# Forward steps taken in pairs, with finer fillers, and 16 small writes moved to another queue

## The chip, the cores and the metric

One core of a Trainium2 chip runs the whole program. The metric is the device time of one execution in microseconds (us); lower is better. The engines are PE (matrix products), DVE (VectorE), ACT (ScalarE, here mostly exponentials), POOL (GpSimd) and SP (SyncE, which here only issues DMAs). Each runs its own instructions in order, and they wait for each other through semaphores.

## What is computed

The reference runs a forward function of two halves and its gradients, in bfloat16, with 2048 positions, width 448 and 16 heads of 28.

```python
# A: linear attention
phi = lambda t: where(t > 0, t + 1, exp(t)) + 1e-6
kv = einsum("bhsd,bhse->bhde", phi(k), v);  z = sum over s of phi(k)
a  = (phi(q) @ kv / (phi(q) . z + 1e-6)) @ wo
# B: softmax attention, 16 query heads, one key and value head
p  = softmax(q @ k.T * 28 ** -0.5);  b = (p @ v) @ wo
out = concatenate([a, b]);  also the gradients of out with respect to all eight inputs, for grad_out
```

## The kernel before

**Forward of B.** The 2048 x 2048 scores of 16 heads are walked in 256 steps, one for each of 4 query blocks of 512, 4 groups of 4 heads, and 16 key tiles of 128 (`steps`, line 872). A step has these parts. `pe_s` (L876; its products are recorded at the helper's line, L105) makes half of a step's scores: two products of 32 rows each, on separate strips of the PE array, into one of two score buffers in PSUM. `act_e` (L888) is the exponential of one half, 128 x 1024, on ACT; a step has two. `pe_o` (L909; recorded at L108) adds the step's four products with the values into `oacc`, on separate column strips, and then issues, on SP's queue, the write of the step's exponentials `e` (512 KB) to DRAM, where the backward reads them again. `e` has five buffers. After every sixteenth step the sum is copied out, and `o_tail` turns it around and divides by the softmax's denominator; after every 64th, `queue_mid` (L930) adds the output product of that query block, the incoming gradient's product and its transposes.

**The order in a step** is written out by hand (L1103 on): both exponentials of step s, both halves of the scores of step s+1, the output products of step s-1, then `block`.

**Fillers.** The whole of the linear-attention half A is cut into pieces (`pieces_A`, L132), each a closure with a cost, close to its PE time in us. `block` (L1072) runs pieces from a list at the end of a step: it has a budget that grows by 1.15 a step up to 1.65, starts a piece while the budget is at least half its cost, and stops before a step's pieces go over the cap of 1.65. Pieces that come from B itself (`fillers`) go first, one a step. A's pieces run in this order: projections with their feature map, which adds exponentials on ACT (steps 17 to 51); the product of keys and input `G_part` (52 to 68); the third phase `p3_*`, output and inner gradients, with much DVE work (70 to 131), in it and behind it `gwo`, the gradient of A's output weight, summed over the four blocks; weight gradients `gw` of the queries (143 to 159); the fifth phase `p5_*`, the input's gradient (160 to 223); `gw` of the keys (224 to 240). Then the pools of A are released and the first tiles of the backward are loaded (`prefetch`).

**PSUM.** Two score buffers, one accumulator, three general buffers (`gen`) that all fillers share.

**DMA queues.** POOL and SP issue DMAs. In the last pass of `gwo` (L388 to 391), each of four groups is added up on DVE and written by four DMAs of 28 rows, 16 in all, on POOL's queue. On the same queue stand the output writes of B (`out_b_sb`, L961, two buffers), its saved output `onat_d` (L952) and A's writes. In the compiled program each DMA of a queue waits for a semaphore that it shares with the one issued eight before it on that queue.

**Backward of B.** 256 units with transposed reads of `e`; it follows the forward, and its code is not touched. A short part with B's weight gradients ends the program.

Of the kernel before, what the change touches and what calls it, by code (L numbers as in the profile page):

```python
# [16 lines left out]
DH = 28  # L17
D = 448
P = 128
# [5 lines left out]
def kernel(  # L25
# [21 lines left out]
    nc = tc.nc  # L47
# [36 lines left out]
    def mm(out_ap, lhsT, rhs, start=True, stop=True):  # L84
        nc.tensor.matmul(out_ap, lhsT=lhsT, rhs=rhs, start=start, stop=stop, tile_position=(0, 0))  # L85
# [46 lines left out]
    def pieces_A(gen, pl, post, flush, pre_tiles, pk_d, early):  # L132
        slabs, halves, w4, accp, chk, small, awk = pl
        out = []

        def piece(cost):
            def add(fn):
                out.append((cost, fn))
                return fn
            return add  # L140

# [234 lines left out]
        def gwo(qc, g):  # L376
            ps = gen([P, D], "gwo_ps")
            for b in range(4):
                mm(ps[:, :], V["onat"][:, qc * 4 + b, g * P:(g + 1) * P], V["ga", qc][:, b, 0:D], start=(b == 0),
                   stop=(b == 3))  # L380
            acc = V["gwo"][:, g, :]
            if qc == 0:
                nc.vector.tensor_copy(out=acc, in_=ps[:, :])
            elif qc < NQC - 1:
                nc.vector.tensor_tensor(out=acc, in0=ps[:, :], in1=acc, op=ALU.add)
            else:
                gsb = awk.tile([P, D], BF16, name="gwoA_sb", tag="osbA", bufs=4)
                nc.vector.tensor_tensor(out=gsb[:], in0=ps[:, :], in1=acc, op=ALU.add)  # L388
                for j in range(4):
                    h = 4 * g + j  # L390
                    nc.gpsimd.dma_start(out_3[h * DH:(h + 1) * DH, :], gsb[32 * j + 1:32 * j + 1 + DH, :])
            if g == 3 and qc < 2:
                ga_load(qc + 2)

# [14 lines left out]
        def part_pk2(k):  # L409
            nc.gpsimd.dma_start(V["onat"][:, 2 * k:2 * k + 2, :].rearrange("p t c -> p (t c)"),  # L410
                                pk_d[:, 1024 * k:1024 * k + 1024])
# [71 lines left out]
        def gw(src, c, q, bi):  # L483
            if q == 0:
                V["acc"] = gen([P, 512], "gw_acc")
            acc = V["acc"]
            for st in range(4 * q, 4 * q + 4):
                mm(acc[:, :], V["x"][:, st, c * P:(c + 1) * P], V[src][:, st, :], start=(st == 0), stop=(st == NS - 1))
            if q == 3:
                out_gw(acc, c, bi)  # L490

        def gw_all(c):
            for q in range(4):
                piece(0.86)(lambda c=c, q=q: gw("gq", c, q, 0))
                if c in (1, 2) and q % 2 == 1:
                    piece(0.0)(lambda k=2 + 2 * c + q // 2: part_pk2(k))

        for c in range(4):
            piece(0.25)(lambda c=c: gwv(c))
# [35 lines left out]
            piece(0.25)(lambda g=g: wT_tr("k", g))  # L535
        gw_all(3)

        def p5_dp(i):
            if i % 4 == 1 and i // 4 < 3:
                xT2(i // 4 + 1)  # L540
            ps = gen([P, 512], "ps_dpk")
            for c in range(4):
                mm(ps[:, :], V["xT", i // 4][:, i % 4, c, :], V["Wp"][:, c, :], start=(c == 0), stop=(c == 3))
            dph = awk.tile([P, 512], BF16, name="dph_A")
            nc.vector.tensor_scalar(out=dph[:], in0=V["pk"][:, i, :], scalar1=-1e-6, scalar2=1.0, op0=ALU.add,
                                    op1=ALU.min)
            gk = awk.tile([P, 512], BF16, name="gk_A", tag="gnd", bufs=4)
            nc.vector.tensor_tensor(out=gk[:], in0=ps[:, :], in1=dph[:], op=ALU.mult)
            V["gk", i] = gk

        def p5_tr(i):
            ps = gen([P, 1024], "qk_ps", BF16)
            tr4(ps, lambda g: V["gq"][:, i, g * P:(g + 1) * P])
            tr4(ps, lambda g: V["pk"][:, i, g * P:(g + 1) * P], 4)
            a = awk.tile([P, 1024], BF16, name="qkT_A", tag="t2k", bufs=4)
            nc.vector.tensor_copy(out=a[:], in_=ps[:, :])
            V["a", i] = a
# [10 lines left out]
        def p5_gx(i, k):  # L568
            a, b = V["a", i], V["b", i]
            if k == 0:  # L570
                V["gx"] = gen([P, D], "ps_gx")
            ps = V["gx"]
            lhs = (a[:, 0:512], b[:], a[:, 512:1024])[k]
            rhs = (V["wT", "q"], V["wT", "k"], V["Z"])[k]
            for g in range(4):
                mm(ps[:, :], lhs[:, g * P:(g + 1) * P], rhs[:, g, :], start=(k == 0 and g == 0),
                   stop=(k == 2 and g == 3))
            if k == 2:
                ot = awk.tile([P, D], BF16, name="gx_sb", tag="osbA", bufs=4)
                nc.vector.tensor_copy(out=ot[:], in_=ps[:, :])  # L580
                nc.gpsimd.dma_start(out1[i * P:(i + 1) * P, :], ot[:])
                del V["a", i], V["b", i]

        for i in range(NS + 2):
            if 0 <= i - 1 < NS:
                piece(0.45)(lambda i=i - 1: p5_tr(i))
            if i < NS:
                piece(0.86)(lambda i=i: p5_dp(i))
            if 0 <= i - 1 < NS:
                piece(0.25)(lambda i=i - 1: p5_tk(i))  # L590
            if 0 <= i - 2:
                for k in range(3):
                    piece(0.76)(lambda i=i - 2, k=k: p5_gx(i, k))
        for c in range(4):
            for q in range(4):
                if q % 2 == 0 and c < 4 and 2 * c + q // 2 in early:
                    piece(0.0)(early[2 * c + q // 2])
                piece(0.86)(lambda c=c, q=q: gw("pk", c, q, 1))
        return out

    ps = ExitStack()
# [267 lines left out]
    def e_rows(g, qc):  # L869
        return (g * NQC + qc) * S  # L870
# [17 lines left out]
    def act_e(h):  # L888
        s, hf = divmod(h, 2)
        if hf == 0:  # L890
# [2 lines left out]
                             in_=sps.pop(h)[:].rearrange("p j (a q) -> p j a q", a=4), func=ACT.Exp,  # L893
                             scale=scale)

    def o_tail(qc, g, osb):
        otp = gen([P, 4, P], "otp")
        for b in range(4):
            tpz(otp[:, b, :], osb[:, b * P:(b + 1) * P], identF)
        otv = otp[:].rearrange("p b (j c) -> p b j c", c=32)  # L900
        rl = rls[qc]
        nc.vector.reciprocal(out=rl[:, :, 4 * g:4 * g + 4], in_=otv[:, :, :, 0])
        for b in range(4):
            nc.vector.tensor_tensor(
                out=hv(onats[qc][:, b, g * P:(g + 1) * P]),
                in0=otv[:, b], in1=rl[:, b, 4 * g:4 * g + 4].unsqueeze(2).to_broadcast([P, 4, 32]),
                op=ALU.mult)

    def pe_o(s):  # L909
        qc, g, t = steps[s]  # L910
        if t == 0:
            oaccs[0] = psAcc.tile([P, 512], F32, name="oacc", tag="acc")
            if g == 0:
                onats[qc] = mid2.tile([P, 4, 512], BF16, name="onat_q")
                rls[qc] = mid2.tile([P, 4, H], F32, name="rl_q")
        oacc = oaccs[0]
        e = es.pop(s)
        for j in range(4):
            cmm(oacc[32 * j:32 * j + 32, :].rearrange("p (a q) -> p a q", a=4), vaug[:, t, :],
                e[:, :, j, :], j, t == 0, t == NS - 1)  # L920
        r0 = e_rows(g, qc) + t * P
        nc.sync.dma_start(edram[r0:r0 + P, :], e[:].rearrange("p a j q -> p (a j q)"))
        if t == NS - 1:
            osb = fwk.tile([P, 512], F32, name="osb")
            nc.vector.tensor_copy(out=osb[:], in_=oacc[:, :])  # L925
            posts.append(lambda: posts.append(lambda: fillers.insert(0, (1.0, lambda: o_tail(qc, g, osb)))))
            if g == 3:
                posts.append(lambda: posts.append(lambda: queue_mid(qc)))

# [142 lines left out]
    def block(rate, cap):  # L1072
        budget[0] = min(budget[0] + rate, cap)
        used = 0.0
        while True:
            q = peek()
            if q is None:
                return
            cost = q[0][0]
            if used > 0 and used + cost > cap or budget[0] < 0.5 * cost:  # L1080
                return
            if q is fillers:
                turn[0] += 1
            q.pop(0)[1]()
            budget[0] -= cost
            used += cost
# [16 lines left out]
    for s in range(NF):  # L1103
        turn[0] = 0
        act_e(2 * s)
        act_e(2 * s + 1)
        pend, posts[:] = posts[:], []
        for fn in pend:
            fn()
        pe_s(2 * s + 2)  # L1110
        pe_s(2 * s + 3)
        if s == NF - 1:
            pe_dp(0)
            pe_dp(1)
        if s > 0:
            pe_o(s - 1)
        block(1.15, 1.65)
        if apools.get("q") == []:
            prefetch(s)
    pe_o(NF - 1)  # L1120
    flush()
    flush()
# [229 lines left out]
```

## Time and profile before

| | |
|---|---|
| median of 3 runs | 1327.22 us (1321.48 to 1327.4) |
| the profiled execution | 1328.86 us, its span 1327.0 us |
| PE, ACT, DVE busy in the span | 1238.0, 1058.0, 938.4 us |
| forward, first to last exponential | 26.65 to 615.76 us, 256 steps |
| backward and end | from there to 1327.0 us |

The rows that carry the argument stand in the prediction. In a row of a group or a timeline the line (L105) is that of the program text, often of a helper; then come engine, operation, output<-inputs, count; in brackets or behind the bar stands the idle time of the engine just before, and what ended it. A row by stage gives each engine's busy time in that stretch with its count of instructions, then the granted PE clock (1.00 is full), the busy share of the DMA engines, and GB/s.

### The profile page before, as it was taken

The page shows a single profiled execution, that of the slowest core. Times are in us where ns is not written, and L with a number is a line of the kernel's source. Part 1 is how long each engine was busy: PE and PEld are TensorE (multiplying, and loading weights), DVE is VectorE, ACT ScalarE, POOL GpSimd, SP SyncE. Part 2 cuts the span into 40 slices and gives each one's busy share as a digit, 9 for nine tenths or more (in the row PEclk, how much of TensorE's full clock was granted, in tenths as well). Part 3 has the DMA queues.
Part 4 walks back from the last instruction along what each step waited for, and adds up shares of the span by engine and source line. Part 5 has one row for each costly group of instructions (what it writes and reads, how often), then busy time and mean ns, then how long its engine had stood idle before and what let it go on. Part 6 is the DMA issues. An engine that isn't in the chain of part 4 may idle for free.

```text
span 1327.0 us, 30124 instructions
## 1 busy us (share of the span) xinstructions
PE 1238.0 (93%) x12604; PEld 589.7 (44%) x12604; DVE 938.4 (71%) x1243; ACT 1058.0 (80%) x1174; POOL 213.9 (16%) x305
## 2 busy tenths in 40 slices
PE   6988998889789999998999999999999999999988
PEld 2322233444333343322555555554555555555544
DVE  6854338888553446212889999998999999999921
ACT  3899987888678888896888888887888888888830
POOL 6400301111411111100031111111111111111110
PEclk8999999999899999995999999998999999999989
DMA  6887798886877787799999999999999999999661
GB/s 171 313 269 280 273 300 302 296 294 264 281 274 293 268 280 296 285 325 309 205 221 206 218 232 222 220 217 224 221 218 220 221 223 217 220 223 218 130 210 46
DMA packets 626312, 322.00 MB, mean 243 GB/s; under 512 B 579120, under 2 KB 585008, under 8 KB 625920
## 3 DMA queue, kind: packets, MB, share of 16 engines
q1 hardware_dynamic: 615072, 291.30, 85.3%
q0 software_dynamic: 10080, 28.73, 6.7%
q8 instruction: 98, 1.61, 0.5%
q14 instruction: 38, 0.31, 0.1%
q10 hardware_dynamic: 1024, 0.05, 0.0%
HBM read 21.87 MB, written 153.45 MB: 132 GB/s over the span
## 4 chain that ended last, share of the span: by engine, by line
PE 66%; DVE 3%; DMA 3%; ACT 3%; issue 2%; POOL 0%; ACTq 0%; DVEq 0%; POOLq 0%
PE dsT_ps L89 19%; PE dp_ps L105 12%; PE akv L108 10%; PE s_ps L105 5%; PE dq_ps L108 4%; PE oacc L108 3%; PE ps_gx L85 3%; PE gw_acc L85 2%; ACT e L892 2%; PE ps_dpk L85 1%; PE gwq_acc L85 1%; ACT dsT L1167 1%; PE gwoB_ps L85 1%; PE ps_gxB L85 1%; DVE ds L1145 1%
## 5 line engine op out<-in xcount | busy, mean ns | idle before, releaser
L1167 ACT ACTIVATE dsT<-dsT_ps 128x1024 bf16<-128x1024 bf16 x512 | 497.5, 1028 | 101.5 <-PE dsT_ps L89 96.0
L892 ACT ACTIVATE e<-s_ps 128x1024 bf16<-128x1024 f32 x512 | 496.8, 1056 | 89.2 <-ACT e L892 50.2
L1145 DVE TENSOR_TENSOR ds<-dp_ps,eN 128x1024 bf16<-128x1024 f32 x336 | 393.1, 1217 | 32.6 <-PE dp_ps L105 24.7
L89 PE MATMUL dsT_ps<-identB,ds 128*128 128x128 bf16 x4096 | 282.5, 221 | 0.5 <-DVE ds L1145 0.2
L89 PEld LDWEIGHTS <-ds 128*128 128x128 bf16 x4096 | 234.5, 98 | 64.0 <-issue 59.9
L1145 DVE TENSOR_TENSOR ds<-dp_ps,eN_h 128x1024 bf16<-128x1024 f32 x176 | 207.0, 1216 | 13.5 <-PE dp_ps L105 7.9
L105 PE MATMUL s_ps<-qT_B,kT_rep 32*128 32x512 bf16 x1024 | 170.4, 398 | 38.6 <-ACT e L892 36.3
L105 PE MATMUL dp_ps<-vT_rep,doT_b 32*128 32x512 bf16 x768 | 151.3, 390 | 7.2 <-DVE ds L1145 6.5
L108 PE MATMUL akv<-ds,qn_b 128*32 128x512 bf16 x1024 | 157.2, 387 | 0.0
L1197 POOL TENSOR_TENSOR dkv<-dkv,asb 128x512 f32<-128x512 f32 x60 | 76.4, 1273 | 493.2 <-ACT asb L1196 493.2
L105 PEld LDWEIGHTS <-kT_rep 32*128 32x128 bf16 x1024 | 43.7, 91 | 166.2 <-issue 155.4
L108 PE MATMUL oacc<-e,vaug 128*32 128x512 bf16 x1024 | 106.3, 406 | 0.8 <-DVE osb L925 0.8
L105 PEld LDWEIGHTS <-doT_b 32*128 32x128 bf16 x768 | 37.1, 91 | 107.5 <-issue 84.3
L108 PE MATMUL akv<-eN,don_b 128*32 128x512 bf16 x512 | 78.4, 386 | 0.0
L108 PE MATMUL dq_ps<-dsT,kn 128*32 128x512 bf16 x1024 | 66.8, 379 | 0.6 <-ACT dsT L1167 0.6
L108 PEld LDWEIGHTS <-vaug 128*32 128x32 bf16 x1024 | 26.5, 93 | 62.3 <-issue 62.3
L105 PE MATMUL dp_ps<-vT_rep,doT_q 32*128 32x512 bf16 x256 | 49.7, 385 | 0.0
L163 DVE TENSOR_SCALAR phi_ex<-phi_ex 128x512 f32<-128x512 f32 x32 | 13.7, 427 | 39.8 <-ACT phi_ex L162 39.8
L580 DVE CAST gx_sb<-ps_gx 128x448 bf16<-128x448 f32 x16 | 10.0, 624 | 44.9 <-PE ps_gx L85 44.9
L108 PEld LDWEIGHTS <-don_b 128*32 128x32 bf16 x768 | 22.0, 94 | 44.1 <-issue 44.1
L108 PEld LDWEIGHTS <-kn 128*32 128x32 bf16 x1024 | 27.8, 97 | 28.2 <-issue 0.4
L108 PE MATMUL akv<-eN_h,don_b 128*32 128x512 bf16 x256 | 39.8, 392 | 0.0
(283 smaller groups left out, 1270.2 us busy)
## 6 DMA issues: line engine op xcount, KB each, us to landing
edram<-e SPq DMA_DIRECT2D x256, 512.0 KB
pk_d<-pkn_A POOLq DMA_DIRECT2D x2, 1024.0 KB, 5.1
onat_d<-onat_q POOLq DMA_DIRECT2D x4, 512.0 KB, 4.5
onat_A<-pk_d POOLq DMA_DIRECT2D x8, 256.0 KB, 4.8
qn_b<-qn_d SPq DMA_DIRECT2D x4, 512.0 KB
onat_B<-onat_d SPq DMA_DIRECT2D x4, 512.0 KB
xa_nat<-in_A_x_dram POOLq DMA_DIRECT2D x1, 1792.0 KB, 12.3
ga_chunk<-in_grad_out_dram POOLq DMA_DIRECT2D x4, 448.0 KB, 6.3
```

What stands on the lines that cost most here:

```text
L85: nc.tensor.matmul(out_ap, lhsT=lhsT, rhs=rhs, start=start, stop=stop, tile_position=(0, 0))
L89: nc.tensor.transpose(out_ps_ap, in_ap, ident[0:k, 0:k], tile_position=(0, 0))
L105: nc.tensor.matmul(out_ap, lhsT=lhsT, rhs=rhs, start=True, stop=True, tile_position=(32 * j, 0))
L108: nc.tensor.matmul(out_ap, lhsT=lhsT, rhs=rhs, start=start, stop=stop, tile_position=(0, 32 * c))
L163: nc.vector.tensor_scalar(out=ex[:], in0=ex[:], scalar1=1.0, scalar2=1e-6, op0=ALU.min, op1=ALU.add)
L580: nc.vector.tensor_copy(out=ot[:], in_=ps[:, :])
L892: nc.scalar.activation(out=es[s][:].rearrange("p a j q -> p j a q")[:, 2 * hf:2 * hf + 2], in_=sps.pop(h)[:].rearrange("p j (a q) -> p j a ...
L1145: nc.vector.tensor_tensor(out=ds[:], in0=dps.pop(h)[:], in1=eNs[i][:, 2 * hf:2 * hf + 2, :], op=ALU.mult)
L1167: nc.scalar.activation(out=dsTs[kcu][:].rearrange("p t j q -> p j t q")[:, 2 * hf:2 * hf + 2, :, b * P:(b + 1) * P], in_=tps.pop(h)[:], fu ...
L1197: nc.gpsimd.tensor_tensor(out=dkv[:, kc * 512:(kc + 1) * 512], in0=dkv[:, kc * 512:(kc + 1) * 512], in1=asb[:], op=ALU.add)
```

## The change

Four things change.

1. The order in the forward. Output products are taken in pairs: in an even step s the products of s-2 and s-1 stand between the two halves of the scores; an odd step has none. The write of `e` becomes a function of its own and is issued for step s-1 right after the exponentials of step s are.
2. Finer pieces. Each piece of `gw` is cut in two, of cost 0.43 instead of 0.86; in the fifth phase `p5_dp` (0.86) becomes two of 0.43, and each of the three `p5_gx` (0.76) two of 0.38. All pieces of these two kinds carry a cap of their own of 1.3.
3. The 16 writes of `gwo` are issued from SP.
4. The cost written for `o_tail` is 0.6 instead of 1.0.

The number of products, exponentials and DMAs stays the same.

```diff
-        def piece(cost):
+        def piece(cost, cap=None):
             def add(fn):
-                out.append((cost, fn))
+                out.append((cost, fn, cap))
...
-                    nc.gpsimd.dma_start(out_3[h * DH:(h + 1) * DH, :], gsb[32 * j + 1:32 * j + 1 + DH, :])
+                    nc.sync.dma_start(out_3[h * DH:(h + 1) * DH, :], gsb[32 * j + 1:32 * j + 1 + DH, :])
...
-            for st in range(4 * q, 4 * q + 4):
+            for st in range(2 * q, 2 * q + 2):
...
-            if q == 3:
+            if q == 7:
                 out_gw(acc, c, bi)
...
-            for q in range(4):
-                piece(0.86)(lambda c=c, q=q: gw("gq", c, q, 0))
+            for q in range(8):
+                piece(0.43, 1.3)(lambda c=c, q=q: gw("gq", c, q, 0))
...
-                piece(0.86)(lambda i=i: p5_dp(i))
+                piece(0.43, 1.3)(lambda i=i: p5_dp0(i))
+                piece(0.43, 1.3)(lambda i=i: p5_dp(i))
...
-                for k in range(3):
-                    piece(0.76)(lambda i=i - 2, k=k: p5_gx(i, k))
+                for k in range(6):
+                    piece(0.38, 1.3)(lambda i=i - 2, k=k: p5_gx(i, k))
...
+    def write_e(s):
+        qc, g, t = steps[s]
+        r0 = e_rows(g, qc) + t * P
+        nc.sync.dma_start(edram[r0:r0 + P, :], es[s][:].rearrange("p a j q -> p (a j q)"))
...
-        r0 = e_rows(g, qc) + t * P
-        nc.sync.dma_start(edram[r0:r0 + P, :], e[:].rearrange("p a j q -> p (a j q)"))
...
-            posts.append(lambda: posts.append(lambda: fillers.insert(0, (1.0, lambda: o_tail(qc, g, osb)))))
+            posts.append(lambda: posts.append(lambda: fillers.insert(0, (0.6, lambda: o_tail(qc, g, osb)))))
...
-            if used > 0 and used + cost > cap or budget[0] < 0.5 * cost:
+            lim = q[0][2] if len(q[0]) > 2 and q[0][2] else cap
+            if used > 0 and used + cost > lim or budget[0] < 0.5 * cost:
...
+        if s > 0:
+            write_e(s - 1)
...
         pe_s(2 * s + 2)
+        if s % 2 == 0 and s > 0:
+            pe_o(s - 2)
+            pe_o(s - 1)
         pe_s(2 * s + 3)
...
-        if s > 0:
-            pe_o(s - 1)
         block(1.15, 1.65)
...
+    write_e(NF - 1)
+    pe_o(NF - 2)
     pe_o(NF - 1)
```

More of the change, by code (lines that the diff above doesn't have):

```diff
@@ L486, in gw @@
             acc = V["acc"]
-            for st in range(4 * q, 4 * q + 4):
+            for st in range(2 * q, 2 * q + 2):
                 mm(acc[:, :], V["x"][:, st, c * P:(c + 1) * P], V[src][:, st, :], start=(st == 0), stop=(st == NS - 1))
-            if q == 3:
+            if q == 7:
                 out_gw(acc, c, bi)
         def gw_all(c):
-            for q in range(4):
-                piece(0.86)(lambda c=c, q=q: gw("gq", c, q, 0))
-                if c in (1, 2) and q % 2 == 1:
-                    piece(0.0)(lambda k=2 + 2 * c + q // 2: part_pk2(k))
+            for q in range(8):
+                piece(0.43, 1.3)(lambda c=c, q=q: gw("gq", c, q, 0))
+                if c in (1, 2) and q % 4 == 3:
+                    piece(0.0)(lambda k=2 + 2 * c + q // 4: part_pk2(k))
         for c in range(4):
@@ L536, in pieces_A, with p5_dp0 @@
         gw_all(3)
-        def p5_dp(i):
+        def p5_dp0(i):
             if i % 4 == 1 and i // 4 < 3:
@@ L541, in p5_dp @@
             ps = gen([P, 512], "ps_dpk")
-            for c in range(4):
-                mm(ps[:, :], V["xT", i // 4][:, i % 4, c, :], V["Wp"][:, c, :], start=(c == 0), stop=(c == 3))
+            for c in range(2):
+                mm(ps[:, :], V["xT", i // 4][:, i % 4, c, :], V["Wp"][:, c, :], start=(c == 0), stop=False)
+            V["dpk"] = ps
+        def p5_dp(i):
+            ps = V.pop("dpk")
+            for c in range(2, 4):
+                mm(ps[:, :], V["xT", i // 4][:, i % 4, c, :], V["Wp"][:, c, :], start=False, stop=(c == 3))
             dph = awk.tile([P, 512], BF16, name="dph_A")
@@ L572, in p5_gx @@
             ps = V["gx"]
-            lhs = (a[:, 0:512], b[:], a[:, 512:1024])[k]
-            rhs = (V["wT", "q"], V["wT", "k"], V["Z"])[k]
-            for g in range(4):
+            lhs = (a[:, 0:512], b[:], a[:, 512:1024])[k // 2]
+            rhs = (V["wT", "q"], V["wT", "k"], V["Z"])[k // 2]
+            for g in range(k % 2 * 2, k % 2 * 2 + 2):
                 mm(ps[:, :], lhs[:, g * P:(g + 1) * P], rhs[:, g, :], start=(k == 0 and g == 0),
-                   stop=(k == 2 and g == 3))
-            if k == 2:
+                   stop=(k == 5 and g == 3))
+            if k == 5:
                 ot = awk.tile([P, D], BF16, name="gx_sb", tag="osbA", bufs=4)
@@ L585, in pieces_A @@
             if 0 <= i - 1 < NS:
-                piece(0.45)(lambda i=i - 1: p5_tr(i))
+                piece(0.45, 1.3)(lambda i=i - 1: p5_tr(i))
             if i < NS:
-                piece(0.86)(lambda i=i: p5_dp(i))
+                piece(0.43, 1.3)(lambda i=i: p5_dp0(i))
+                piece(0.43, 1.3)(lambda i=i: p5_dp(i))
             if 0 <= i - 1 < NS:
-                piece(0.25)(lambda i=i - 1: p5_tk(i))
+                piece(0.25, 1.3)(lambda i=i - 1: p5_tk(i))
             if 0 <= i - 2:
-                for k in range(3):
-                    piece(0.76)(lambda i=i - 2, k=k: p5_gx(i, k))
+                for k in range(6):
+                    piece(0.38, 1.3)(lambda i=i - 2, k=k: p5_gx(i, k))
         for c in range(4):
[L595 to L598, printed above, removed]
+            for q in range(8):
+                if q % 4 == 0 and 2 * c + q // 4 in early:
+                    piece(0.0)(early[2 * c + q // 4])
+                piece(0.43, 1.3)(lambda c=c, q=q: gw("pk", c, q, 1))
         return out
```

## The prediction

> **What bounds the kernel now.** I read the page first (busy shares, the clock line), then busy time by stage, then a short timeline of single steps, then the groups and waits of the score products.
>
> ```profile
> span 1327.0 us, 30124 instructions
> PE 1238.0 (93%) x12604; PEld 589.7 (44%) x12604; DVE 938.4 (71%) x1243; ACT 1058.0 (80%) x1174; POOL 213.9 (16%) x305
> PEclk8999999999899999995999999998999999999989
> ```
> ```profile
> core 0: us, PE busy (x) PEld busy (x) DVE busy (x) ACT busy (x) POOL busy (x), PEclk, DMA share, GB/s
> 27.00:147.00 120.00, 105.28 (x686) 36.29 (x686) 74.62 (x160) 109.56 (x133) 22.45 (x29) 0.96 0.76 277
> 148.00:184.00 36.00, 34.54 (x218) 11.31 (x215) 7.33 (x18) 32.54 (x35) 12.95 (x23) 0.95 0.83 308
> 184.00:330.00 146.00, 129.63 (x1145) 60.25 (x1143) 117.66 (x245) 119.02 (x125) 22.96 (x50) 1.00 0.84 289
> 330.00:376.00 46.00, 36.95 (x275) 15.68 (x274) 28.84 (x59) 29.83 (x32) 16.92 (x33) 0.89 0.81 275
> 376.00:552.00 176.00, 164.70 (x1269) 67.70 (x1268) 76.09 (x159) 149.91 (x159) 28.00 (x49) 1.00 0.79 284
> 552.00:590.00 38.00, 34.88 (x218) 10.99 (x217) 5.63 (x12) 35.77 (x39) 2.70 (x5) 1.00 1.00 308
> 590.00:616.00 26.00, 22.57 (x110) 5.14 (x109) 1.14 (x5) 24.47 (x26) 0.00 (x0) 0.51 1.02 360
> 632.00:1290.00 658.00, 648.24 (x8324) 352.28 (x8317) 595.46 (x521) 540.90 (x610) 91.31 (x78) 0.99 1.07 215
> ```
> PEclk8999999999899999995999999998999999999989
>
> ```profile
> 202.72 0.40 PE L105 MATMUL s_ps<-qT_B,kT_rep 32*128 32x512 bf16 x4
> 203.05 0.40 PE L108 MATMUL oacc<-e,vaug 128*32 128x512 bf16 x4
> 203.20 3.77 ACT L892 ACTIVATE e<-s_ps 128x1024 bf16<-128x1024 f32 x4 [0.66 <-ACT e L892]
> 204.35 0.39 PE L105 MATMUL s_ps<-qT_B,kT_rep 32*128 32x512 bf16 x2
> 205.19 0.39 PE L105 MATMUL s_ps<-qT_B,kT_rep 32*128 32x512 bf16 x2 [0.46 <-ACT e L892]
> 205.51 0.40 PE L108 MATMUL oacc<-e,vaug 128*32 128x512 bf16 x4
> ```
> Columns: start, length, engine, instruction, count, idle before it. At 202.72 PE came late: both score buffers were free, all four score products ran side by side in 0.40 us, and PE passed on after 0.33; ACT had idled 0.66 and started 0.48 after the scores did. At 204.35 PE came early: the first two products ran, and the other two had to wait until 205.19 for ACT to read the second buffer, 0.84 later. So either ACT waits for PE or PE waits between the halves of a step. From ACT's row, (3.77-1.02)/3 = 0.92 us is the pace of exponentials (one alone takes about 1.02); the second ends at 203.20+0.92+1.02 = 205.14, and the scores follow 0.05 later. ACT alone could do a step in 1.84.
>
> ```profile
> L105 PE MATMUL s_ps<-qT_B,kT_rep 32*128 32x512 bf16 x1024 | 170.4, 398 | 38.6 <-ACT e L892 36.3
> ```
> How much that spread costs over the whole forward: if the four products ran together in each of 256 steps, their busy time would be 256 x 0.40 = 102; it is 170.4. The excess of 68 and the 36.3 us of waiting make 104 us, 0.41 a step, or 0.82 in two steps.
>
> **The change part by part.**
>
> *Pairs.* An even step becomes scores, two rounds of output products, scores, fillers; an odd step scores, scores, fillers. Two rounds together are priced by the end of the forward, where they already stand so, at half clock:
>
> ```profile
> 613.98 0.61 PE L105 MATMUL s_ps<-qT_B,kT_rep 32*128 32x512 bf16 x2 [0.25 <-ACT e L892]
> 614.52 0.62 PE L108 MATMUL oacc<-e,vaug 128*32 128x512 bf16 x4
> 616.35 1.04 PE L108 MATMUL oacc<-e,vaug 128*32 128x512 bf16 x8
> ```
> Four more products add 0.42 at a clock of about 0.51, so 0.21 at full clock: 0.33+0.21 = 0.54 for two rounds, where two single ones take 0.66. Beside fillers, two steps cost PE now 2 x (0.33+0.33) + 0.82 = 2.14. After: 0.33+0.54+0.33 in the even step, whose wait of up to 0.92 is covered by 0.87 of work, and 0.33 plus the odd step's own wait. That is 1.53 plus a wait that ACT sets. I follow it for the stage of the fifth phase:
>
> ```profile
> 376.00:552.00 176.00, 48.76 (x316) 149.91 (x159) 1.00 0.79 284
> PE s_ps L105 <- ACT e L892: 10.5, 32, 0.5
> ```
> (busy time of the score products there, and PE's waits for ACT.) 316 products are 79 steps: 48.76-79 x 0.40 = 17.2, with 10.5 of waits 27.7, or 0.35 a step. Fillers take 2.21-0.35-0.66 = 1.20. New order, from an even step's first scores at 0: second scores at 0.87, fillers 1.20 to 2.40. Exponentials start at 0.48 and 1.40 and end at 1.50 and 2.42. Odd step: scores at 2.40 and, after the second exponential, 2.47; fillers to 4.00. Its exponentials start at 2.88 and 3.80; the last ends at 4.82. Next pair: scores at 4.00 and 4.87, fillers to 6.40; exponentials from 4.72 and 5.64, the second until 6.66; odd scores at 6.40 and 6.71, fillers to 8.24. So 8.24 in four steps, 2.06 each, against 2.21: 0.15. The old order followed in the same way gives 2.16, so 0.10 is the lower reading. Smaller pieces fill about 1.15 us a step more evenly, and in the order of the compiled program the linear-attention half's last filler stands in step 232, before in 240; a denser filling makes the earlier steps a little longer. I take 0.13 for the 100 steps from 132 to 232: **13 us**. For steps 3 to 15 and 52 to 68, with coarse pieces as before, 0.10 each: 30 steps, 3 us. In 27:147 the stage also gives ACT the feature-map exponentials (109.56 of 120 busy): nothing for steps 16 to 51.
>
> Steps 69 to 130 (184:330) have VectorE busy 117.66 of 146, and PE also waits for it:
>
> ```profile
> PE ps_oa L85 <- DVE gndT_A L342: 6.0, 6, 1.1
> ```
> A faster PE meets that wait more often. Ends: 0 and 62 x 0.10 = 6; I take 3, the middle, since waits and spread are of one size there.
>
> *The 16 writes.* The stage 330:376 took 46 us for 16 steps, 10.6 over 16 x 2.21.
>
> ```profile
> 340.32 4.02 POOL L391 DMA_DIRECT2D out_dram<-gwoA_sb  x8 [4.28 <-DVE gwoA_sb L388]
> 349.12 2.01 POOL L391 DMA_DIRECT2D out_dram<-gwoA_sb  x4
> 353.54 1.00 POOL L391 DMA_DIRECT2D out_dram<-gwoA_sb  x2 [0.87 <-DMA onat_d<-onat_q]
> 354.53 0.55 POOL L961 DMA_DIRECT2D out_dram<-out_b_sb  x1
> 355.57 0.62 DVE L939 CAST out_b_sb<-ps_ob 128x448 bf16<-128x448 f32 x1 [6.62 <-DMA out_dram<-out_b_sb]
> 356.24 1.65 PE L85 MATMUL ps_ob<-woB_pr,oTq 128*128 128x448 bf16 x4 [4.93 <-DVE out_b_sb L939]
> 359.38 1.94 ACT L892 ACTIVATE e<-s_ps 128x1024 bf16<-128x1024 f32 x2 [6.37 <-issue]
> out_dram<-gwoA_sb POOLq DMA_DIRECT2D x16, 24.5 KB, 4.4
> ```
> The 16 issues of 0.50 us fill POOL's queue from 340 to 354. In the compiled program each DMA of this queue also waits for the landing of the one eight before it, and one lands 4.4 us after its issue. The attention output's writes stand behind; it has two buffers, so VectorE waits 6.62 for a landing, PE 4.93, ACT 6.37; the clock falls to 0.89 of full over the stage. With the writes on SP, POOL loses 8 us of issues just there. Ends: 4.93, PE's one stop, and 10.6; VectorE's heavy products of the same stage remain. I take **9 us**.
>
> SP pays for it with waits for VectorE's sums, behind which the writes of e queue:
>
> ```profile
> SPq L922 <- ACT e L892: 386.0, 223, 7.9
> ```
> SP stood waiting for ACT on 223 of 256 writes of e, 386 us. That hides 16 issues. If a write of e slips by one landing, 4.4 us, it still has its five buffers: the tile is reused four steps, 8.8 us, later. I take nothing; the other end is rival 3. The write of e is now issued apart from the output products and still waits for ACT only: nothing, both ways. The lower cost written for the transposes after each sixteenth step (1.0 to 0.6) only lets the planner add pieces there.
>
> *The tail.* From step 233, not 241, steps hold only scores and output products. Clock there now: 0.51 (590:616). At that clock scores hold PE 0.54 (613.98 to 614.52) and two output rounds 0.54+0.42, so an even step has 1.50 between its scores, more than the 0.92 of one exponential: the second starts up to 0.58 late. ACT's lag absorbs part; over 11 pairs between 0 and 6 us lost, I take **-3**. The Trainium skill (TensorE: Matmul & The Clock Gate, Part 1, The HAM clock gate) says that the clock halves after an idle window of about 3.4 us; by it the tail would keep full clock and this term would be 0. The trace disagrees: 0.51 with PE busy 22.57 of 26 us.
>
> *Sum:* 13+3+3+9-3 = 25. The profiled execution took 1328.86 us (span 1327.0 and 1.9 around it): 1304. The median shown, 1327.22, is 1.6 lower: **1302**; I round to 1303.
>
> **Rivals.**
>
> 1. *Only the stall goes.* The even step's wait goes and comes back in the odd one, or VectorE and ACT absorb it. For it: ACT busy 149.91 of 176 is the busiest after PE. Against: 1.84 leaves 0.37 a step. 1327-9 = 1318.
> 2. *Slower: the four strips lose their company.* In the even step two score products run alone. Where PE is late anyway, two steps cost 1.53 against 1.32, 0.21 more. It decides from the point where the present spread falls under 0.21 in two steps. Over all 127 pairs that is 27; less the stall's 9, 1327+18 = 1345. Against: the measured spread is 0.82 in two steps. The Trainium skill (TensorE: Matmul & The Clock Gate, Part 3, Packing small matmuls) says that four row tiles finish in the time of one matmul plus about 4 ns each; by that rule the split costs a matmul time per pair, which is this rival. The trace agrees on the packing (0.40 for four, 0.39 for two), and the spread says that it is seldom used.
> 3. *SP's queue becomes the wait.* Sixteen writes in about three steps, with waits for VectorE and landings. Four groups of one landing are 17.6; buffers absorb some 5 to 9, so ACT would stall about 10: 1313.
>
> **How the numbers follow.** Forecast 0.70, rival 1 0.15, rival 2 0.06, rival 3 0.09. Low end: 10.6 for the stall, 15+3+6 for pairs, no tail loss: 35 less than 1327, and 1293 with a us of rounding. High end: it takes in rivals 3 and 1 with some loss in the tail: 1320. Rival 2 stays outside. About 0.5% (6.6 us) is what a measurement can tell from no change. Faster: forecast, rival 3 mostly and two thirds of rival 1, 0.86; within 0.5%: the rest of rival 1 and the mild end of rival 2, 0.08; slower 0.06.
>
> **What would show it.** Right: the stage of the fifth phase near 2.06 us a step, score products split in even steps only with little wait; no VectorE wait of several us on the attention output's landing; the clock line full around 26 to 28% of the span; the backward's length unchanged. Wrong: odd steps with waits near 0.9 (rival 1), steps longer than 2.21 with ACT idle (rival 2), ACT waiting on a write of e near the 16 writes (rival 3), or a tail above 2.15 us a step.

## The result and the profile after

The changed kernel took 1310.05 us (median of 4 runs, 1304.89 to 1313.16) against 1327.31 for the kernel before beside it (1321.48 to 1336.39): a ratio of 0.984, with a 95% interval of 0.981 to 0.988. The forecast was 1303 with a range of 1293 to 1320. The profiled execution took 1308.03 us against 1328.86.

One remark for the reader of the prediction: its step times are read from ACT's counts in the stage rows, two exponentials a step. 159 in 176 us are 79.5 steps of 2.21, 125 in 146 us are 2.34 each, 32 in 46 are 2.88, 26 in 26 are 2.00.

The page of the changed kernel, with the lines that answer to those shown of before:

```profile
span 1306.3 us, 30065 instructions
PE 1223.2 (94%) x12548; PEld 583.4 (45%) x12604; DVE 938.0 (72%) x1243; ACT 1056.9 (81%) x1174; POOL 206.4 (16%) x289
PEclk9999998999999999956999999999999999999989
L105 PE MATMUL s_ps<-qT_B,kT_rep 32*128 32x512 bf16 x1024 | 185.5, 403 | 27.5 <-ACT e L899 24.0
```

The score products are spread more (185.5 us busy, before 170.4), as they must be when something stands between their halves, and PE waits for ACT 24.0 instead of 36.3 us. What the pairs save shows in the output products, first before, then after, on the two pages:

```profile
L108 PE MATMUL oacc<-e,vaug 128*32 128x512 bf16 x1024 | 106.3, 406 | 0.8 <-DVE osb L925 0.8
```
```profile
L108 PE MATMUL oacc<-e,vaug 128*32 128x512 bf16 x1024 | 84.2, 408 | 0.0
```

Two rounds now stand side by side, 22 us less busy time. To see where the time went, the forward is cut at steps, not at times: at the first exponential of steps 64, 128, 152, 224 and 232, and at the end of the last. These are the stages before and then after (start and end, length, then busy time of PE, PEld, DVE, ACT, POOL with counts, clock, DMA share, GB/s):

```profile
175.31:326.53 151.22, 134.57 (x1174) 61.90 (x1173) 117.24 (x245) 122.76 (x128) 22.06 (x48) 1.00 0.83 286
326.53:389.96 63.43, 52.67 (x400) 22.05 (x399) 37.82 (x78) 45.65 (x48) 20.83 (x41) 0.92 0.81 264
389.96:551.61 161.65, 151.88 (x1174) 62.95 (x1173) 70.41 (x145) 137.17 (x145) 24.99 (x44) 1.00 0.79 289
551.61:567.59 15.98, 14.71 (x94) 4.75 (x91) 3.08 (x8) 15.11 (x16) 1.08 (x2) 1.00 0.94 282
567.59:615.76 48.17, 42.94 (x236) 11.41 (x236) 3.69 (x9) 45.52 (x49) 1.62 (x3) 0.74 1.03 345
```
```profile
173.49:328.58 155.09, 138.92 (x1189) 63.99 (x1201) 123.66 (x257) 123.21 (x129) 26.45 (x57) 0.98 0.83 282
328.58:385.11 56.53, 51.35 (x393) 20.85 (x397) 34.32 (x74) 45.72 (x49) 11.19 (x20) 0.97 0.95 321
385.11:534.40 149.29, 146.26 (x1123) 58.94 (x1136) 65.78 (x134) 136.58 (x144) 22.87 (x40) 1.00 0.84 302
534.40:551.22 16.82, 16.29 (x106) 5.54 (x106) 3.61 (x9) 15.19 (x17) 1.63 (x3) 1.00 1.07 317
551.22:602.02 50.80, 37.63 (x205) 8.02 (x206) 2.45 (x7) 45.69 (x48) 0.54 (x1) 0.58 0.88 311
```

Third phase (steps 64 to 128): 3.9 us longer. The stage with the stall (128 to 152): 6.9 shorter. Query gradients and fifth phase (152 to 224): 12.4 shorter, 2.245 to 2.07 us a step, with PE busy 146.26 of 149.29. Tail (224 on): 3.5 longer. With 1.5 in the first 64 steps the forward is 13.3 us shorter, 589.1 to 575.8. What follows it, whose code is the same, is 7.1 shorter, 711.3 to 704.2. The stages don't hold quite the same work as before: by the counts of weight loads (PEld), 37 products fewer stand in steps 152 to 224 and 28 more in 64 to 128. A few steps of the fifth phase after:

```profile
403.12 0.39 PE L105 MATMUL s_ps<-qT_B,kT_rep 32*128 32x512 bf16 x2
403.44 0.61 PE L108 MATMUL oacc<-e,vaug 128*32 128x512 bf16 x8
403.99 0.39 PE L105 MATMUL s_ps<-qT_B,kT_rep 32*128 32x512 bf16 x2
404.31 1.04 PE L85 MATMUL ps_dpk<-Wp_A,xaT 128*128 128x512 bf16 x3
405.19 0.39 PE L89 MATMUL gkT_ps<-identB,gk_A 128*128 128x128 bf16 x4
405.50 0.56 PE L105 MATMUL s_ps<-qT_B,kT_rep 32*128 32x512 bf16 x4
```

The even step is as drawn in the prediction: 0.32, 0.55 and 0.32, and no idle time in brackets. The odd step's four scores stand together, within 0.56. PE's waits for ACT in that stage after:

```profile
PE s_ps L105 <- ACT e L899: 0.3, 2, 0.2
```

They were 10.5 us; with 146.26 of 149.29 us busy, PE is now the bound there.

### The profile page after: what moved, and what is told of

It is laid out like the page before. It is cut to its first block, busy times and chain, and to the rows that moved or that the text cites. A ratio compares the mean times of both kernels' runs of the same rounds, so it can differ in the third digit from the quotient of the medians.

```text
span 1306.3 us, 30065 instructions
## 1 busy us (share of the span) xinstructions
PE 1223.2 (94%) x12548; PEld 583.4 (45%) x12604; DVE 938.0 (72%) x1243; ACT 1056.9 (81%) x1174; POOL 206.4 (16%) x289
## 4 chain that ended last, share of the span: by engine, by line
PE 65%; issue 4%; DVE 3%; DMA 3%; ACT 2%; POOL 1%; DVEq 0%; ACTq 0%; POOLq 0%
PE dsT_ps L89 19%; PE dp_ps L105 12%; PE akv L108 10%; PE s_ps L105 5%; PE dq_ps L108 4%; PE ps_gx L85 3%; PE oacc L108 3%; PE gw_acc L85 2%; ACT e L899 1%; PE gwq_acc L85 1%; PE gwoB_ps L85 1%; PE ps_dpk L85 1%; ACT dsT L1183 1%; DMA out_dram<-out_b_sb 1%; PE ps_gxB L85 1%
## 5 line engine op out<-in xcount | busy, mean ns | idle before, releaser
L105 PE MATMUL s_ps<-qT_B,kT_rep 32*128 32x512 bf16 x1024 | 185.5, 403 | 27.5 <-ACT e L899 24.0
L108 PE MATMUL akv<-ds,qn_b 128*32 128x512 bf16 x1024 | 156.3, 385 | 0.0
L105 PEld LDWEIGHTS <-kT_rep 32*128 32x128 bf16 x1024 | 50.6, 91 | 188.2 <-issue 178.6
L108 PE MATMUL oacc<-e,vaug 128*32 128x512 bf16 x1024 | 84.2, 408 | 0.0
L935 DVE COPY osb<-oacc 128x512 f32<-128x512 f32 x16 | 11.0, 687 | 48.8 <-PE oacc L108 48.6
```

The costliest lines, as they stand in the source:

```text
L105: nc.tensor.matmul(out_ap, lhsT=lhsT, rhs=rhs, start=True, stop=True, tile_position=(32 * j, 0))
```

## The experiments

Each kernel starts from the one before or from the changed one. Where the time of a kernel lies is read from the starts of the exponentials in its trace, as above; all stage times, in us, stand in one table (forward: first exponential's start to the last one's end; behind: from there to the end of the span). The ratio comes from several executions, the stage times from one, the profiled execution.

| kernel | ratio to before, 95% interval | steps 64-128 | 128-152 | 152-224 | 224-end | forward | behind |
|---|---|---|---|---|---|---|---|
| before | 1 | 151.2 | 63.4 | 161.6 | 64.2 | 589.1 | 711.3 |
| after | 0.984 (0.981 to 0.988) | 155.1 | 56.5 | 149.3 | 67.6 | 575.8 | 704.2 |
| e1, writes on SP only | 0.9945 (0.9922 to 0.9968) | 151.4 | 57.8 | 161.6 | 64.1 | 583.2 | 704.9 |
| e2, pairs only | 0.9927 (0.9905 to 0.9948) | 150.3 | 63.2 | 156.3 | 63.5 | 580.1 | 710.2 |
| e3, finer pieces only | 0.9982 (0.9962 to 1.0003) | 151.4 | 62.0 | 155.7 | 66.6 | 583.9 | 710.9 |
| e4, after, writes on POOL | 0.9957 (0.9935 to 0.9979) | 155.4 | 62.6 | 149.1 | 67.9 | 582.3 | 713.2 |
| e5, after, gwv later | 0.9876 (0.9848 to 0.9903) | 155.5 | 57.6 | 148.8 | 68.1 | 577.2 | 709.7 |
| e6, after, old order in the tail | 0.9836 (0.9805 to 0.9868) | 155.4 | 56.7 | 148.7 | 65.2 | 575.7 | 701.7 |
| e7, after, cost 1.0 | 0.9851 (0.9819 to 0.9883) | 150.1 | 59.8 | 149.2 | 67.0 | 571.2 | 702.0 |
| e8, e5 and e7 | 0.9833 (0.9798 to 0.9868) | 150.1 | 59.6 | 149.0 | 67.3 | 571.7 | 708.4 |
| e9, e6 and e7 | 0.985 (0.983 to 0.9871) | 149.7 | 61.3 | 149.3 | 65.0 | 570.4 | 713.2 |
| e10, e9 and dearer small pieces | 0.9853 (0.9834 to 0.9873) | 150.1 | 55.4 | 149.9 | 67.2 | 569.7 | 709.8 |
| e11, e9, writes on POOL | 0.9902 (0.9878 to 0.9925) | 150.1 | 64.1 | 149.0 | 65.3 | 575.4 | 714.7 |
| e12, before once more | one run | 151.4 | 63.4 | 161.6 | 64.3 | 587.4 | 711.4 |

**e1: the writes alone.** The kernel before with

```diff
-                    nc.gpsimd.dma_start(out_3[...], gsb[...])
+                    nc.sync.dma_start(out_3[...], gsb[...])
```

> The kernel before with only the 16 writes issued from SP. Theory 1 (the prediction: the writes on POOL's queue cause the 10.6 us excess around 330 to 376): 9 us less, about 1318, and VectorE's 6.6 us wait for the landing of the attention output's write is gone. Rival (the writes only carry the wait with them to SP and to the four buffers that they share with other outputs): 0 to 4 us less, 1323 to 1327, with a new wait of several us of VectorE for a landing in that stage.

1321.33 against 1329.04. Steps 128 to 152 fall by 5.6 us, more than the rival's 4 and less than theory 1's 9:

```profile
328.08:385.87 57.79, 49.57 (x400) 21.31 (x399) 38.12 (x78) 45.64 (x48) 12.83 (x25) 1.00 0.88 296
```

The clock in that stage is 1.00 instead of 0.92, and POOL has lost 8 us of issues. So the writes on POOL did cause the larger part of the stall. VectorE's wait of 6.62 for the landing of the attention output is gone, as theory 1 said; the rival's new wait of VectorE came only at 1.2 us. But ACT has a wait in this stage that the kernel before doesn't have at all, for writes of `e` that stand on SP's queue among the 16:

```profile
ACT e L892 <- DMA edram<-e: 4.2, 4, 1.6
```

That is rival 3 of the prediction, at 4.2 us.

**e2: the pairs alone.** The kernel before with the new order in the loop and `write_e`, as in the change's diff; nothing else.

> The kernel before with only the new order (output products in pairs between the halves of the scores, the write of e issued apart); coarse pieces, writes on POOL. Theory 1: about 0.10 us a step less in the steps 132 to 232 and 48 to 68, nothing in the others, 2 to 4 us lost in the tail: 1315 to 1320. Rival (two strips alone cost a product's time per pair of steps and the gain of the whole change is that of the finer pieces): 0 to 27 us more, 1327 to 1354, with the fifth phase at 2.21 us a step or above.

1318.0 against 1329.04. In 152 to 224 the step falls from 2.245 to 2.17, 5.3 us, with coarse pieces:

```profile
386.47:542.76 156.29, 150.94 (x1171) 62.05 (x1171) 69.70 (x145) 136.69 (x145) 25.04 (x44) 1.00 0.83 301
```

That is 0.07 a step, less than the 0.10 expected. The rival of the lost strips is out: pairs gain with whole pieces too, and the stage with the stall hardly changes (0.2). The 2 to 4 us that were expected to be lost in the tail were not: from step 224 on it is 0.7 shorter.

**e3: the finer pieces alone.** The changed kernel with the old order, the writes on POOL and the cost at 1.0; the write of `e` stays a function of its own.

> The kernel before with only the finer pieces and their cap; old order, writes on POOL, old cost of the transposes. Theory 1: evener filling is worth at most 0.05 us a step in the 80 steps of weight gradients and fifth phase: 0 to 4 us less, 1323 to 1327. Rival (the finer pieces carry the gain): 8 to 14 us less, 1313 to 1319, with the fifth phase at 2.10 us a step or below.

1325.82 against 1329.04, in theory 1's range; but the stage shows more than the total:

```profile
388.60:544.35 155.75, 148.82 (x1136) 60.18 (x1135) 68.75 (x142) 138.27 (x145) 23.26 (x41) 1.00 0.81 297
```

5.9 us less in 152 to 224, 0.08 a step. Not all of it is gain: PE is busy 148.82 us there instead of 151.88, with 1136 products instead of 1174, and 36 more products stand behind step 224, where the kernel gives back 2.4. From step 152 to the end 3.5 us are left, 0.05 a step. In the stage itself the two add: 5.3+5.9 = 11.2 of the 12.4.

**e4: the writes back.** The changed kernel with the first diff reversed.

> The changed kernel with the 16 writes back on POOL. Theory 1: the stall of the kernel before returns beside the gains of the new order: 5 to 9 us above the changed kernel, 1315 to 1319. Rival (the wait is in the shared buffers and in the landing, whichever queue issues): within 3 us of the changed kernel, 1307 to 1313.

1323.83 against 1329.04. Beside the changed kernel's ratio that is 1.1%, some 15 us, more than theory 1 gave. In the profiled executions 6.1 lie in steps 128 to 152, where a stall is back with the clock at 0.86, and 9 behind the forward:

```profile
331.56:394.18 62.62, 55.03 (x396) 22.12 (x396) 34.75 (x74) 45.91 (x49) 19.17 (x36) 0.86 0.85 287
```

It is not the same stall. The lower cost has moved the 16 writes from steps 134 to 139 to steps 128 to 131, and VectorE now waits 8.0 us for their own landings, of tiles that share four buffers with the next outputs, and 1.4 for the attention output's.

**What is left of the stall: e5.** In the changed kernel SP, DVE, PE and ACT show this at steps 129 to 132:

```profile
333.66 4.42 SPq L391 DMA_DIRECT2D out_dram<-gwoA_sb  x8
...
337.95 1.23 DVE L458 CAST gwA_sb<-gwv_ps 128x448 bf16<-128x448 f32 x2 [2.97 <-DMA out_dram<-gwA_sb]
...
338.63 0.38 PE L85 MATMUL Wp_ps<-dkvzT_blk,wTv_A 128*128 128x128 bf16 x4 [2.31 <-DVE gwA_sb L458]
...
341.35 1.94 ACT L899 ACTIVATE e<-s_ps 128x1024 bf16<-128x1024 f32 x2 [4.37 <-PE s_ps L105]
```

The last eight writes keep SP 4.42 us, where POOL needed 4.02 for eight; the first eight took SP 1.67 and 2.02 for four each. The tiles that they read share four buffers with the next outputs, and VectorE waits 2.97 for a landing; by the row it is that of one of those next outputs (`gwA_sb`, issued on POOL), while the other buffers are still held. e5 moves those next outputs away:

```diff
-        for c in range(4):
-            piece(0.25)(lambda c=c: gwv(c))
...
         for g in range(4):
             piece(0.25)(lambda g=g: Zf(g))
+        for c in range(4):
+            piece(0.25)(lambda c=c: gwv(c))
```

> The changed kernel with the four small value-weight gradients (gwv) placed behind the four Z pieces instead of ahead of Wp; nothing else. Theory (the stall of 4.4 us that is left at step 132 is VectorE waiting for a buffer of the four that the output-weight gradient's tiles still hold until their writes land): steps 128 to 136 fall from 22.0 us to 17 to 18, 4 to 5 us less in all. Rival (VectorE and PE are simply overloaded in these steps): within 1.5 us of the changed kernel, and the wait stands a step or two later.

1312.91: not better. Steps 128 to 136 do fall, from 22.0 to 18.5, but 136 to 152 rise from 34.6 to 39.2. That is the rival's "a step or two later", though not by its cause. VectorE waits for no landing in this stage any more, and ACT now waits for SP's work:

```profile
ACT e L899 <- DMA edram<-e: 5.0, 2, 4.0
ACT e L899 <- DMA out_dram<-gwoA_sb: 1.5, 1, 1.5
```
```profile
348.62 2.31 SPq L956 DMA_TRANSPOSE gbT_q<-in_grad_out_dram  x1
351.03 3.30 SPq L906 DMA_DIRECT2D edram<-e  x4
354.50 7.09 SPq L152 DMA_TRANSPOSE xaT<-pqT_A  x1
361.69 9.87 SPq L906 DMA_DIRECT2D edram<-e  x7
```

A transposed load holds SP's queue for 7.09 us, seven writes of `e` come only behind it, and ACT runs out of `e` buffers. So rival 3 of the prediction exists in this stage. Here it comes through a transposed load, in e1 among the 16 writes; the changed kernel shows no wait of ACT for a write of `e` in steps 128 to 152.

**e6: the tail.** The changed kernel; where the list of pieces is empty, the output products stand again behind both halves of the scores.

```diff
-        if s % 2 == 0 and s > 0:
-            pe_o(s - 2)
-            pe_o(s - 1)
+        if s > 0:
+            due.append(s - 1)
+        old = apools.get("q") == []
+        while due and s % 2 == 0 and not old:
+            pe_o(due.pop(0))
         pe_s(2 * s + 3)
...
+        while due and old:
+            pe_o(due.pop(0))
...
```

> The changed kernel with the old order (output products of the step before, behind both halves of the scores) once the list of pieces is empty, so from step 233. Theory of the prediction (at half clock two output rounds between the halves starve ACT): steps 232 to 255 fall from 48.4 us by 2 to 3. Rival (the tail costs more because the filling ends eight steps earlier and the clock is halved for longer, whichever order): within 1 us.

From step 232 on it takes 48.4 us instead of 50.8, 2.4 less, so the order is most of the tail's loss of 3.5. In the total (1306.96) that can't be told from the changed kernel, and its first 64 steps took 2.5 more.

**e7: the cost.** The changed kernel with `fillers.insert(0, (1.0, ...))`.

> The changed kernel with the cost written for the transposes after each sixteenth step back at 1.0. Theory (the stall in steps 80 to 88, 24.0 us where the kernel before and the kernel with pairs alone have 20.6 and 21.0, comes from pieces moved against VectorE's heavy products by that cost): 20.6 to 21.5 us in these steps, 2 to 3 us less in all. Rival (pairs and finer pieces together cause it): 23 to 24 us there, no difference in all.

Steps 80 to 88 take 20.7 us instead of 24.0, and 64 to 128 take 150.1 instead of 155.1: the theory holds for these steps. But 128 to 152 take 59.8 instead of 56.5, and in the total (1310.18) no gain can be told; the profiled execution (1302.11) was the shortest of its six. With the dearer cost the 16 writes stand at steps 134 to 138 again, and ACT waits 2.7 us for writes of `e`. What the dearer cost avoided was this, in the changed kernel:

```profile
217.86 1.01 PE L368 MATMUL dkvz_ps<-gnd_A,oq_A 128*128 128x128 bf16 x8 [1.39 <-DVE gndT_A L342]
...
219.37 0.61 PE L105 MATMUL s_ps<-qT_B,kT_rep 32*128 32x512 bf16 x2
...
220.07 1.02 ACT L899 ACTIVATE e<-s_ps 128x1024 bf16<-128x1024 f32 x1 [2.45 <-issue]
```

PE stops for VectorE; the granted clock is 0.50 from 217.8 to 224.6, so that two score products take 0.61 instead of 0.39, and ACT loses 2.45.

**e8: e5 and e7 together.**

> The changed kernel with the gwv pieces behind Z and the transposes' cost at 1.0. If both theories hold, the gains add: 6 to 8 us below the changed kernel. If only one holds, its gain alone. The length of the backward tells besides whether it goes with the queue of the 16 writes: 703 to 706 us in the two kernels with them on SP so far, 710 to 713 in the four with them on POOL; if that is chance, these four kernels, all with SP, will show both lengths.

1307.99: within its spread of the changed kernel. The gains do not add: steps 128 to 152 take 59.6, as in e7. The last sentence of the expectation is answered: with the writes on SP the part behind the forward came out at both lengths, 701.7 to 709.7 in these four.

**e9, e10, e11: the combinations.** e9 has the edits of e6 and e7. e10 adds

```diff
-            piece(0.25)(lambda c=c: gwv(c))
+            piece(0.6)(lambda c=c: gwv(c))
```

and the same for `Wp` and `Zf`. e11 is e9 with the writes on POOL.

> The changed kernel with the transposes' cost at 1.0 and the old order in the tail. From the stages measured apart (about 2 us each in the profiled executions): steps 64 to 152 about 210 us, steps 240 to 255 about 29.5, and 2 to 4 us below the changed kernel. If the two changes only move waits about, the same as the changed kernel.

> As e9, and the 12 pieces gwv, Wp and Z carry a cost of 0.6 instead of 0.25, so that two instead of four stand in a step. Theory (the stall that stays in steps 128 to 152 in every variant is VectorE, with some 0.65 us of copying for each of these pieces): these steps fall from about 60 us to 52 to 54, 6 us in all. Rival (in that stage the transposes on SP hold back the writes of e, and ACT waits for e's buffers at a DMA share of 1.0 and more): 57 to 61 us, no difference beyond 2 us in all.

> As e9 with the 16 writes on POOL. If the queue of the writes decides both a stall around step 136 and part of the backward: 10 to 16 us above e9, with a backward of 710 to 713 us. If the backward's length is chance: 4 to 7 us above e9, with a backward anywhere from 701 to 713.

e9: 1308.07, the same as the changed kernel; the forward is 5.4 us shorter, the part behind it 8.9 longer. In steps 128 to 152 it shows rival 3 most plainly: from 335.28 to 349.45, while SP issues the 16 writes and two transposed loads, it issues only three writes of `e`, and ACT waits:

```profile
ACT e L899 <- DMA edram<-e: 6.8, 4, 2.1
```

e10: 1309.11; steps 128 to 152 fall from 61.3 to 55.4, near the 52 to 54 of the VectorE theory and below the rival's 57 to 61. Neither is the whole of it: a wait of ACT of 3.2 us at 367.34 in e9 is gone, and 4.0 of its 6.8 us for writes of `e` are left. The total does not fall: 2.1 come back in the tail, into which the dearer pieces push work, and the first 64 steps took 1.9 more. e11: 1314.85, 6.8 above e9, within the 4 to 7 that were expected if the length behind the forward is chance; the profile has 5.0 more in the forward and 1.5 behind it (714.7, a little above both expectations).

**e12: the kernel before again.**

> The kernel before, unchanged, for a second profile. If the backward's length goes with the queue of the writes: 710 to 713 us. If it is chance, it may come out anywhere from 701 to 713. The forward's stages should repeat within about 1 us each.

The stages repeat within 0.3 us from step 64 on, and behind the forward it is 711.4 again. No version beats the changed kernel by more than its measurement is uncertain: e6 to e10 have shorter forwards or the same, and totals inside its interval.

## Why the prediction was right, and where its sum was off

**Pairs and finer pieces, 100 steps from 132, forecast 13 us: right in mechanism and near in size.** The worked order gave 2.06 us a step; 2.07 was measured, and PE's waits of 10.5 us became 0.3, as the step-by-step working said. In 72 of those steps alone 12.4 us went, 0.17 a step where 0.13 was taken; 37 of the stage's products stand elsewhere now, so a part of that is work moved, not saved. The forecast gave the finer pieces 0.03 or so of it; e3 shows 0.08 in the stage and 0.05 with what it gives back behind step 224. ACT's idle time in the stage fell from 24.5 to 17.5 us in e3; how much of that is the evener filling and how much the smaller load, no run separates.

**The first 64 steps, forecast 3: not resolved.** 1.5 less, but the repeat of the kernel before was 2.0 less than its first profile.

**The third phase, forecast 3 us of gain: wrong, 3.9 us of loss.** The failed step is the sentence that the lower cost "only lets the planner add pieces there". It moved pieces onto VectorE's densest steps, VectorE's busy time in the stage rose from 117.24 to 123.66 us, and the clock fell to 0.98. With the cost at 1.0 (e7 to e11) this stage takes 149.7 to 150.1 us, about 1.3 less than before: pairs bring a little here, less than the 3 taken. The same cost worked the other way in the next stage: with 0.6 the 16 writes are issued by step 131, and steps 128 to 152 take 56.5 us; with 1.0 and the writes on SP (e7, e8, e9) they take 59.6 to 61.3.

**The 16 writes, forecast 9: right in cause, mis-sized.** The stage went down 6.9 in all, 5.6 by the writes alone (e1), 6.1 with the rest in place (e4). The step that was mis-sized is "I take nothing" for SP's queue. Its argument was that `e` has five buffers; but in e1, with nothing else changed, ACT waits 4.2 us for writes of `e`, and in e7, e8, e9 and e10 2.7 to 6.8. In the changed kernel, where the lower cost has moved the writes to steps 128 to 131, that wait is absent; what is left there is a landing that holds shared buffers (2.97 us of VectorE's wait). With pieces in other places a transposed load on SP holds back the writes of `e` (e5).

**The tail, forecast -3: right.** 3.5 lost from step 224 on, 2.6 of them from step 232 on, of which 2.4 by the order (e6). The clock was 0.58 from step 232 on, and at 560.25 us the halves of an even step's scores started 1.52 us apart, 1.50 in the working. With pairs alone (e2), whose clock was 0.78 there, the tail lost nothing; that points to the order and the longer stretch at half clock together.

**Behind the forward, forecast no change: 7.1 less in the profile; where it went is shown, what started it is open.** Two things differ. One is late tiles of `e` in the backward, 6.8 us of VectorE's waits before and 4.1 after:

```profile
DVE ds L1145 <- DMA eN<-edram: 3.7, 2, 2.9
DVE ds L1145 <- DMA eN_h<-edram: 3.1, 2, 2.3
```
```profile
DVE ds L1161 <- DMA eN<-edram: 3.3, 2, 2.7
DVE ds L1161 <- DMA eN_h<-edram: 0.8, 1, 0.8
```

The other is the clock. Before, it falls to half with the latest of these tiles; after, it stays full from 613.7 to 1265.7:

```profile
918.20:925.10 6.90, 6.17 (x46) 3.69 (x45) 5.38 (x5) 3.22 (x4) 1.27 (x1) 0.51 1.17 254
```
```profile
613.70:1265.70 652.00, 646.04 (x8347) 351.25 (x8349) 596.41 (x522) 542.29 (x612) 91.43 (x78) 1.00 1.09 218
```

The half clock of the tail also lasts 15.8 us into the part behind the forward before, 11.7 after. Together that is 11 us less at half clock, worth by estimate at most half of that, 5.5, and 2.7 us less of waits, where 7.1 went. The other kernels fit: between 632 and 1260 us of their spans the two with the shortest part (e6 and e7, 701.7 and 702.0) have at most one late tile and no half clock, the three with the longest (e4, e9, e11) 7 to 13 us of late tiles and 10 to 14 us of half clock.

What makes a tile late is not shown. With the writes on POOL the length was 710.2 to 714.7 in six profiles; with them on SP it was 701.7 to 713.2 in eight. The ranges overlap, so the queue does not decide it alone. But in the three pairs of kernels that differ in the queue only, SP is shorter each time (e1 and before 6.4, after and e4 9.0, e9 and e11 1.5), so the queue may well shift the odds; three pairs are few, and no run names the way.

In sum: the forecast's 25 us in the forward were 13.3; the third phase (7 off) and the stage of the writes, whose 9 and the pairs' share of 20 steps made 11.6 where 6.9 came, explain the rest. That the total came as near as it did is in part luck: 7.1 us came from the part that the forecast left alone.

## What to carry to other kernels

Where one engine alternates with another through two buffers, look between the two halves of its step for a wait that other work of the same kind can fill, and price it by the spread between the halves, not by the idle time alone. A planner's cost is a position: changing one moves pieces, and the DMAs that they issue, against every other engine's load, and has to be followed there. A stage that got shorter may have lost work to its neighbours, so count the instructions beside the time. Moving small writes to another queue helps the queue that they leave; on the new one, what stands behind them waits, and the buffers that they read from are held until they land.

## What the runs showed that was not expected

Sixteen small writes on SP's queue kept ACT waiting 4.2 us for writes of `e` (e1), although the tiles have five buffers. A transposed load held SP's queue 7.09 us (e5), and the writes behind it made ACT wait too. The clock stayed near half in the whole tail although PE's longest single idle time there was about 1 us after the change and 0.6 before it. And a late tile in the backward cost more than its wait: before, VectorE waited 2.9 us for one until 917.65, and the clock stood at half from 918.2 to 925.1.
